# Loading the last columns of w_out first, one 8 KB row per DMA engine, in a decode step of attention and gated MLP

## The chip, the cores and the metric

The kernel runs on one core of one Trainium2 chip. The core has five engines with instruction queues of their own: TensorE (PE in the profile; its weight loads are PEld), VectorE (DVE), ScalarE (ACT), GpSimd (POOL) and SyncE (SP). Data move between the chip's memory (HBM) and the on-chip buffer by 16 DMA engines. SyncE and ScalarE issue the transfers here, each through a queue of its own; the profile calls SyncE's queue q1 and ScalarE's q10.

The metric is the device time of one execution in microseconds (us). The kernel before takes 678.6 us, the median of three runs that lie between 678.34 and 678.68.

## The reference

For eight sequences (B = 8), one new token each, with D = 512:

```
xn  = layernorm(x)
q   = xn @ wq                                   # 512 x 4096: 32 heads of 128
s   = softmax(q k^T / sqrt(128)) v  @ wo        # 8 kv heads, 4096 cached keys and values
z   = gelu(xn @ w_in)                           # 512 x 1792
z1, z2 = halves of z;  z2 = layernorm(z2) * w_sp + b_sp
g   = silu((z1 * z2) @ w_out)                   # 896 x 512
out = x + s * g
```

All of it is 32-bit floating point. The caches of keys and values are 128 MiB each, wq and wo 8 MiB each, w_in and w_out about 5.4 MB together.

## The kernel before

**Slots.** The on-chip buffer holds three slots, A, B and C, of 128 partitions x 64 KB (8 MiB each). Every large operand goes through a slot as one transfer of 128 rows of 64 KB: wq into B, then for each of the eight kv heads the first half of its keys into A, the second half into B, the first half of its values into C, the second half into B, and at the end wo into A in seven pieces (`WO_PIECES`). In the program's list the transfers of keys and values stand at lines 591 and 596, with 597 for the last quarter of the last values, and wo at 601; SyncE issues all of them in this order. A transfer into a slot is issued as soon as TensorE has made the last matmul that reads what the slot held. While SyncE waits for that, the transfers behind it in its queue wait too.

**The start.** ScalarE issues x in two halves of 8 rows (line 362) and then `w_mlp` (line 368), which holds w_in and nearly all of w_out: 128 rows of 41,984 bytes into slot C. SyncE issues wq (line 365), then `w_ext` (line 371), then the first keys (591). `w_ext` is what is missing from `w_mlp`: the last 256 columns (XN) of the last 128 rows of w_out, 128 KB. It is packed by the host: the 128 rows are cut into XC chunks of XK rows, and each partition of the transfer holds one row of every chunk side by side. Before, XK = 32 and XC = 4, so it is 32 partitions of 4 KB, seen as 8 groups (XG) of 4 rows (XR). An extra row of zeros that stands between the groups in HBM and is not loaded keeps them apart.

**The work at the start.** x is normalised (lines 419 to 427), transposed, and multiplied by wq in `project_q` (447 to 455) into the queries of all heads; this frees slot B. Then `mlp` computes the gate: w_in (469), gelu and the normalisation on VectorE and ScalarE (473 to 499), two transposes of the product (502), XC transposes of the rows that meet `w_ext` (509), the matmuls with w_out from `w_mlp` (514), and XC matmuls with `w_ext` (518). Line 518 is the last to read slot C, so the first values wait for it. Lines 520 to 531 finish the gate.

**The loop.** For each kv head: scores of the 8 sequences against both halves of the keys (550), the softmax (554 to 573), the products with the values (582 to 585), a combining matmul (588). After the eighth head wo is applied as its pieces land (609, 617), and the result is multiplied by the gate, added to x and stored (663 to 665).

**What sets the order.** Each engine executes in program order. A recorder derives the waits from which tile regions are read and written; a transfer has a semaphore that reaches 16 when all parts of it have landed.

Of the kernel before, what the change touches and what calls it, by code (L numbers as in the profile page):

```python
# [16 lines left out]
B, D = 8, 512  # L17
HKV, REP, S, DH = 8, 4, 4096, 128
NK = D // P
# [3 lines left out]
FH = 896  # L23
FQ = 256
NB = FH // P
# [11 lines left out]
E = 2  # L37
W = P // E
BANK = 512
XG, XR, XN = 8, 4, 256  # L40
XK = XG * XR
XC = P // XK
LAST = NB - 1
# [303 lines left out]
def gqa_gmlp_decode(real, x, kT, v, wq, wo, w_mlp, w_ext, out):  # L347
    nc = Recorder(real)

    def sb(name, shape, **kw):  # L350
        return real.alloc_sbuf_tensor(name, shape, F32, **kw).ap()
# [4 lines left out]
    slots = {n: sb(f"slot_{n}", [P, SLOT], align_bytes=ALIGN) for n in "ABC"}  # L356
    pbuf = sb("pbuf", [P, J * P])
    tbuf = sb("tbuf", [P, B * J * G * REP])

    xs_sb = pbuf[:B, :XW]  # L360
    for c in range(0, XW, XW // X_PARTS):
        nc.scalar.dma_start(xs_sb[:, c:c + XW // X_PARTS], x[:, c:c + XW // X_PARTS])
    x_sb = xs_sb[:, :D]

    nc.sync.dma_start(slots["B"], wq, key="B")
    wq_sb = slots["B"].rearrange("p (k n) -> p k n", k=NK)
    n_in, n_mlp = NK * 2 * FH, NK * 2 * FH + NB * D - XN
    nc.scalar.dma_start(slots["C"][:, :n_mlp], w_mlp, key="C")
    w_in_sb = slots["C"][:, :n_in].rearrange("p (k n) -> p k n", k=NK)
    ext = slots["C"][:XK, n_mlp:n_mlp + XC * XN]  # L370
    nc.sync.dma_start(ext, w_ext[:, :XR])
    w_ext_sb = ext.rearrange("p (c d) -> p c d", d=XN)

    def w_out_sb(j):
        return slots["C"][:, n_in + j * D:min(n_in + (j + 1) * D, n_mlp)]
# [163 lines left out]
    p = pbuf.rearrange("p (j s) -> p j s", j=J)  # L539
# [163 lines left out]
```

## Time and profile before

| quantity | value |
|---|---|
| median of three runs | 678.6 us (678.34 to 678.68) |
| the profiled execution | 678.58 us, of which the span from first to last instruction is 677.3 us |
| bytes read from HBM | 290.74 MB, 429 GB/s over the span |
| mean busy share of the DMA engines | 90% or more in 39 of 40 slices, 70 to 80% in the last |
| TensorE busy | 374.1 us (55%) |
| VectorE busy | 165.1 us (24%) |
| mean granted TensorE clock | 0.773 |
| packets of q1 / q10 | 6088 with 285.38 MB / 176 with 5.39 MB |

A row of a timeline has the start in us from the start of the span, the time it takes in us, engine, line, operation and tiles. SPq and ACTq are the instruction queues of SyncE and ScalarE, where issuing a transfer is an instruction of its own. The DMA view, asked for a short stretch, counts the packets that start in that stretch by queue; the percentage behind a queue is the time of those packets as a share of 16 engines over the stretch, so it passes 100% where long packets start in a short stretch. A row of a transfer is one packet; a packet of 4 bytes is the note by which one DMA engine tells the semaphore that its part is done. Such notes are the packets under 512 bytes.

### The profile page before, as it was taken

The numbers are of one execution on the slowest core, as the hardware profiler recorded it, in microseconds if no ns is written. First come the engines' busy times: TensorE is split into PE (matmuls) and PEld (weight loads), VectorE is DVE, ScalarE is ACT, GpSimd is POOL, SyncE is SP. The second block draws the span as 40 slices with busy tenths as digits, with TensorE's granted clock in tenths as the row PEclk, the third lists the DMA queues.
The fourth block names the chain that finished last, engine by engine and source line by source line (L and its number), as shares of the span: only waits on it lengthen the run. The fifth ranks groups of instructions, "written<-read, shape, count | busy, mean of one in ns | idle before, by whom it ended". The sixth has DMA issues, their size and how long they took to land. (4 is left out here: it accounts for less than half of the span.)

```text
span 677.3 us, 6190 instructions
## 1 busy us (share of the span) xinstructions
PE 374.1 (55%) x2670; PEld 120.4 (18%) x2670; DVE 165.1 (24%) x262; ACT 15.0 (2%) x35; POOL 4.4 (1%) x22
## 2 busy tenths in 40 slices
PE   0084865446665454555754464655745356655576
PEld 0031221112211121111211121111211021111222
DVE  2014133301430033401431024401422024400451
ACT  0000000000000000000000000000000000000000
POOL 1000000000000000000000000000000000000000
PEclk9996767787876667887676778877667788876688
DMA  9999999999999999999999999999999999999997
GB/s 383 435 438 434 434 434 431 434 434 437 434 434 434 434 434 434 434 434 434 434 434 434 434 434 434 434 437 434 437 441 434 434 437 434 434 437 434 427 419 310
DMA packets 6270, 290.86 MB, mean 429 GB/s; under 512 B 840, under 2 KB 856, under 8 KB 1528
## 3 DMA queue, kind: packets, MB, share of 16 engines
q1 hardware_dynamic: 6088, 285.38, 97.4%
q10 hardware_dynamic: 176, 5.39, 1.8%
q8 instruction: 5, 0.08, 0.0%
q14 instruction: 1, 0.01, 0.0%
HBM read 290.74 MB, written 0.03 MB: 429 GB/s over the span
## 5 line engine op out<-in xcount | busy, mean ns | idle before, releaser
L550 PE MATMUL sc<-slot_B,qz 128*32 128x512 f32 x512 | 72.0, 725 | 70.9 <-PEq L550 70.9
L582 PE MATMUL o_ps<-slot_B,tbuf 128*16 128x512 f32 x512 | 75.3, 715 | 62.7 <-PEq L582 62.7
L550 PE MATMUL sc<-slot_A,qz 128*32 128x512 f32 x512 | 73.8, 741 | 45.6 <-PEq L550 45.6
L582 PE MATMUL o_ps<-slot_C,tbuf 128*16 128x512 f32 x512 | 75.7, 732 | 12.6 <-PEq L582 12.6
L584 DVE TENSOR_TENSOR o_all<-o_ps,diag 128x512 f32<-128x512 f32 x64 | 44.2, 691 | 133.2 <-DVEq L584 133.2
L554 DVE TENSOR_REDUCE nm<-sc 128x1 f32<-128x1024 f32 x8 | 9.8, 1225 | 266.2 <-DVEq L554 266.2
L585 DVE TENSOR_REDUCE o_sb<-o_all 128x128 f32<-128x512 f32 x64 | 67.7, 1058 | 9.3
L550 PEld LDWEIGHTS sc<-slot_B,qz 128*32 128x32 f32 x512 | 19.9, 130 | 122.8 <-issue 122.8
L550 PEld LDWEIGHTS sc<-slot_A,qz 128*32 128x32 f32 x512 | 20.2, 133 | 92.7 <-issue 92.7
L588 PE MATMUL po<-fold,o_sb 128*128 128x4 f32 x128 | 24.2, 259 | 18.8 <-PEq L588 17.4
L588 PEld LDWEIGHTS po<-fold,o_sb 128*128 128x128 f32 x128 | 19.9, 195 | 74.3 <-issue 74.3
L582 PEld LDWEIGHTS o_ps<-slot_B,tbuf 128*16 128x16 f32 x512 | 13.4, 105 | 90.5 <-issue 90.1
L582 PEld LDWEIGHTS o_ps<-slot_C,tbuf 128*16 128x16 f32 x512 | 15.5, 112 | 53.8 <-issue 53.5
L572 PE MATMUL scr<-ident,pbuf 128*128 128x128 f32 x64 | 15.5, 424 | 13.4 <-PEq L572 13.4
L447 PE MATMUL scr<-slot_B,xnT 128*32 128x512 f32 x64 | 9.7, 761 | 19.1 <-PEq L447 19.1
L572 PEld LDWEIGHTS scr<-ident,pbuf 128*128 128x128 f32 x64 | 12.6, 224 | 13.8 <-issue 13.8
L555 ACT ACTIVATE pbuf<-sc,nm 128x1024 f32<-128x1024 f32 x8 | 8.9, 1113 | 273.5 <-DVEq L554 273.5
L573 DVE COPY tbuf<-scr 128x512 f32<-128x512 f32 x16 | 11.1, 691 | 12.4 <-DVEq L573 12.4
L558 PE MATMUL scr<-ident,nm 128*1 128x128 f32 x8 | 2.2, 269 | 13.7 <-PEq L558 13.7
L449 DVE TENSOR_SCALAR pbuf<-scr 128x512 f32<-128x512 f32 x2 | 1.4, 691 | 28.0 <-PE scr L447 28.0
L609 PE MATMUL sc<-slot_A,oT 128*8 128x512 f32 x48 | 7.8, 729 | 0.8 <-DMA slot_A<-in_wo 0.8
L565 PE MATMUL scr<-wl,same 128*128 128x1 f32 x16 | 3.6, 297 | 8.0 <-PEq L565 8.0
(105 smaller groups left out, 83.4 us busy)
## 6 DMA issues: line engine op xcount, KB each, us to landing
slot_B<-in_v SPq DMA_DIRECT2D x1, 6144.0 KB, 25.4
slot_C<-in_w_mlp ACTq DMA_DIRECT2D x1, 5248.0 KB, 35.8
slot_A<-in_wo SPq DMA_DIRECT2D x1, 3584.0 KB, 36.4
slot_B<-in_v SPq DMA_DIRECT2D x1, 2048.0 KB, 28.3
slot_A<-in_wo SPq DMA_DIRECT2D x1, 2048.0 KB, 40.8
slot_A<-in_wo SPq DMA_DIRECT2D x2, 768.0 KB, 42.9
slot_A<-in_wo SPq DMA_DIRECT2D x1, 512.0 KB, 44.3
slot_A<-in_wo SPq DMA_DIRECT2D x2, 256.0 KB, 44.6
```

Source lines behind the costliest of these rows:

```text
L447: nc.tensor.matmul(pq[R * g:R * (g + 1), :], xnT[:, k, :], wq_sb[:, k, lo:lo + REP * DH], start=(k == 0), stop=(k == NK - 1))
L550: nc.tensor.matmul(sc[R * g:R * (g + 1), c, :], qz[:, b * R:(b + 1) * R], k_sb[:, i, c, g, :], start=(b == 0), stop=(b == B - 1))
L554: nc.vector.tensor_reduce(nm, sc, op=ALU.max, axis=AX.XY, negate=True)
L555: nc.scalar.activation(p.rearrange("p j s -> p (j s)"), sc.rearrange("p c s -> p (c s)"), AF.Exp, bias=nm, accum_out=l)
L565: nc.tensor.matmul(tot, same_all, wl, start=True, stop=True)
L572: nc.tensor.transpose(t[:, j * P:(j + 1) * P], p[:, 4 * c + j, :], ident)
L573: nc.vector.tensor_copy(pT[:, :, 4 * c:4 * c + 4].rearrange("p b j (g r) -> p (j g) b r", g=G), t.rearrange("p (m b r) -> p m b r", b=B, r ...
L582: nc.tensor.matmul(of[R * c:R * c + G * REP, :], pT[:, b, j, :], v_unit[:, j], start=(j < G), stop=(j >= J - G))
L584: nc.vector.tensor_mul(o_all[b % 2], o, diag[:, :, None].to_broadcast([P, G, DH]), after=after)
L585: nc.vector.tensor_reduce(o_sb[b % 2], o_all[b % 2].rearrange("p g d -> p d g"), op=ALU.add, axis=AX.X)
L588: nc.tensor.matmul(po[:, b * REP:(b + 1) * REP], o_sb[b % 2], fold, start=True, stop=True)
L609: nc.tensor.matmul(part[R * r:R * r + B, :], oT[:, h, r, :], wo_sb[:, m, :], start=(m < REP), stop=(m >= FOLDED - REP))
```

## The change

ScalarE issues `w_ext`, and does so first of all, ahead of x and `w_mlp`. SyncE's queue has wq and behind it at once the first keys. `w_ext` is cut differently: XG, XR = 16, 1 in place of 8, 4, so that it is 16 partitions of 8 KB (XK = 16, XC = 8) with the same 128 KB. With that the loops over XC at lines 507 to 509 and 517 to 518 make 8 transposes and 8 matmuls of 16 rows in place of 4 and 4 of 32 rows.

```diff
-XG, XR, XN = 8, 4, 256
+XG, XR, XN = 16, 1, 256
 XK = XG * XR
 XC = P // XK
...
+    nc.sync.dma_start(slots["B"], wq, key="B")
+    wq_sb = slots["B"].rearrange("p (k n) -> p k n", k=NK)
+    n_in, n_mlp = NK * 2 * FH, NK * 2 * FH + NB * D - XN
+    ext = slots["C"][:XK, n_mlp:n_mlp + XC * XN]
+    nc.scalar.dma_start(ext, w_ext[:, :XR])
+    w_ext_sb = ext.rearrange("p (c d) -> p c d", d=XN)
+
     xs_sb = pbuf[:B, :XW]
     for c in range(0, XW, XW // X_PARTS):
         nc.scalar.dma_start(xs_sb[:, c:c + XW // X_PARTS], x[:, c:c + XW // X_PARTS])
     x_sb = xs_sb[:, :D]
-
-    nc.sync.dma_start(slots["B"], wq, key="B")
-    wq_sb = slots["B"].rearrange("p (k n) -> p k n", k=NK)
-    n_in, n_mlp = NK * 2 * FH, NK * 2 * FH + NB * D - XN
     nc.scalar.dma_start(slots["C"][:, :n_mlp], w_mlp, key="C")
     w_in_sb = slots["C"][:, :n_in].rearrange("p (k n) -> p k n", k=NK)
-    ext = slots["C"][:XK, n_mlp:n_mlp + XC * XN]
-    nc.sync.dma_start(ext, w_ext[:, :XR])
-    w_ext_sb = ext.rearrange("p (c d) -> p c d", d=XN)
```

The first place is the start of ScalarE's list. A row names the line, the operation, the tile written and the one read, and the partitions x elements of each.

```order
-L362 DMA pbuf<-in_x 8x288 x2
-L368 DMA slot_C<-in_w_mlp 128x10496
+L364 DMA slot_C<-in_w_ext 16x2048
+L369 DMA pbuf<-in_x 8x288 x2
+L371 DMA slot_C<-in_w_mlp 128x10496
 L477 ACT_TABLE_LOAD
 L477 ACTIVATE pbuf<-pbuf 128x512
```

`w_ext` now stands ahead of both halves of x and of `w_mlp`; line numbers moved by the edit.

The second place is TensorE's list at the end of `mlp`, from the last sum of the normalisation to the matmuls behind w_out.

```order
 L484 MATMUL scr<-var_sum,same 128x1
 L502 MATMUL scr<-ident,pbuf 128x128 x2
-L509 MATMUL scr<-ident,pbuf 32x32 x4
+L509 MATMUL scr<-ident,pbuf 16x32 x8
 L514 MATMUL sc<-slot_C,tbuf 32x512 x6
 L514 MATMUL sc<-slot_C,tbuf 32x256
-L518 MATMUL sc<-slot_C,tbuf 32x256 x4
+L518 MATMUL sc<-slot_C,tbuf 32x256 x8
 L525 MATMUL scr<-tbuf,same 32x64 x8
```

There are four transposes and four matmuls more, all ahead of the point at which slot C is free.

## The prediction

> **What bounds the kernel now.** I read the page's row of DMA shares first, then the chain that ended last, then the last stretch in small windows.
>
> ```profile
> DMA  9999999999999999999999999999999999999997
> DMA slot_A<-in_wo 7%; PE sc L550 1%; SPq L601 0%; PE sc L617 0%; SPq L597 0%; DVE res L663 0%; DVE res L664 0%; PEldq L550 0%
> ```
>
> The 16 DMA engines are busy from start to end, and the chain's largest piece is the landing of wo. No engine's arithmetic bounds the time: only the bytes, the rate, the few us before the first packet and behind the last one, and any moment in which a DMA engine has no row to fetch. The columns of the next view are stretch and length in us, busy time of PE, PEld, DVE, ACT and POOL, granted clock, DMA share and GB/s.
>
> ```profile
> 672.50:674.00 1.50, 1.25 (x88) 1.11 (x76) 0.00 (x0) 0.00 (x0) 0.00 (x0) 1.00 0.44 161
> 674.00:675.00 1.00, 0.79 (x44) 0.54 (x32) 0.00 (x0) 0.00 (x0) 0.00 (x0) 1.00 0.02 8
> 674.70 0.43 PE L617 MATMUL sc<-slot_A,oT_end 128*32 128x64 f32 x16 [0.21 <-DMA slot_A<-in_wo]
> ```
>
> The engines don't end together. After 672.5 each has on average 1.5 x 0.44 + 1.0 x 0.02 = 0.68 us of work, so a perfectly even load would end near 673.2; the last matmuls start at 674.70, when the last engine is done. Evening out the engines can therefore bring at most 1.5 us, and less if the engine that ends last is not the one relieved. Where the unevenness comes from can be counted in the landing of one transfer of keys late in the run (first 594.5 to 595.8, then 595.8 to 597.0; 40 slices each), with the instruction loads between 45 and 110 us behind it:
>
> ```profile
> DMA  0000000090990900900000990900000009000000
> DMA packets 22, 0.72 MB, mean 555 GB/s; under 512 B 11, under 2 KB 11, under 8 KB 11
> DMA  0000000000900090000900000900000900000000
> ...
> q8 instruction: 3, 0.05, 0.3%
> ```
>
> Eleven engines note their end in the first stretch (two of the nines stand for two engines each): six at 594.76 to 595.02, five at 595.22 to 595.57. Five follow at 596.10 to 596.73. An instruction load goes to one engine and delays it alone, which is my reading of the five late ones. The gap between the six and the five is what an uneven small transfer leaves.
>
> **The change part by part.**
>
> *The bytes of w_ext per engine.* These are DMA views of 31.0 to 31.8 us, and of 34.4 to 35.4 us:
>
> ```profile
> q1 hardware_dynamic: 8, 0.03, 9.9%
> ...
> DMA packets 47, 1.05 MB, mean 1049 GB/s; under 512 B 16, under 2 KB 16, under 8 KB 32
> q1 hardware_dynamic: 39, 1.05, 243.0%
> q10 hardware_dynamic: 8, 0.00, 0.5%
> ```
>
> Eight rows of 4 KB take 9.9% of 16 x 0.8 us, which is 0.158 us each. In the second view 16 notes end: 8 are q10's, the others q1's notes for w_ext. So eight engines carry it, four rows each: 0.63 us more than the other eight. They also carry x's 16 rows (below). The change gives every engine two times 4 KB, 0.32 us: these eight end 0.32 us earlier, the others 0.32 us later, the mean stays. In the landing above, six plus two of the late five would be the engines without w_ext, five plus three those with it, the last among them. Then the last goes from 596.73 to 596.41, while the later of the other two late ones, near 596.22, comes to 596.54. **The end moves by 596.54 - 596.73 = -0.2 us**; the bounds are -0.32 us (all late ones relieved) and +0.32 us (the last is one without w_ext).
>
> [...]
>
> *The turns at the start.* The stretches are 7.2 to 7.9 and 9.6 to 10.4 us, and then comes the use of x:
>
> ```profile
> DMA packets 24, 0.87 MB, mean 1242 GB/s; under 512 B 0, under 2 KB 8, under 8 KB 8
> q10 hardware_dynamic: 16, 0.35, 114.5%
> ...
> DMA packets 16, 0.52 MB, mean 655 GB/s; under 512 B 8, under 2 KB 8, under 8 KB 8
> q1 hardware_dynamic: 8, 0.52, 151.1%
> ...
> 10.64 0.68 DVE L419 BATCH_NORM_STATS2 st<-pbuf 8x6 f32<-8x512 f32 x1 [6.98 <-DMA pbuf<-in_x]
> ```
>
> A row of wq takes 151.1% of 16 x 0.8 us by eight, 2.42 us. At 7.2 us eight engines make x's second rows, while the other eight already make w_mlp's first; at 9.6, one row of wq later, x's eight notes. So each engine alternates between the two queues row by row, and a note costs a turn of 2.42 us like a row. With w_ext ahead, x's first half comes a place later, so on x's engines two more turns (its row and its note) stand before w_mlp: about 4.8 us. x is in use at 15.5 in place of 10.6 us. That is covered by wq, which TensorE can't have before 33.69 (next fence). Of the eight rows that w_mlp has on each of these engines, the first four now go beside wq's fifth to eighth and the rest beside the 4 KB rows of w_ext. After the change the first two go beside wq's seventh and eighth, two follow there, and five rows of the first keys come between the rest and its note: + 5 x 2.42 - 3 x 0.16 + 0.32 = 11.9 us.
>
> ```profile
> 33.69 6.07 PE L447 MATMUL scr<-slot_B,xnT 128*32 128x512 f32 x32 [19.05 <-PEq L447]
> 47.43 3.65 PE L469 MATMUL scr<-slot_C,xnT 128*32 128x256 f32 x64 [1.16 <-DVE scr L463]
> ...
> 62.10 0.39 PE L509 MATMUL scr<-ident,pbuf 32*32 32x32 f32 x4
> 66.13 1.91 PE L518 MATMUL sc<-slot_C,tbuf 32*32 32x256 f32 x8
> 71.29 9.48 PE L550 MATMUL sc<-slot_A,qz 128*32 128x512 f32 x64 [2.04 <-PEq L550]
> 80.58 7.05 PE L550 MATMUL sc<-slot_B,qz 128*32 128x512 f32 x64
> ```
>
> The eight engines in question end their part of w_mlp between 34.4 and 35.4 now: that view has their notes. These would come at 46.3 to 47.3. TensorE can begin line 469 at 47.43 + 0.32 (wq lands later by w_ext's share) = 47.75. It fits, by 0.4 us at the worst: the cover is project_q, and one turn more costs 2.42 us less that 0.4.
>
> *The matmuls.* Line 518 doubles: 8 records, 1.91 us, so +1.91 (up to +3.8 should the clock be half there). Line 509 gets four more transposes, about +0.2. The copy at line 510 stays beside line 514's matmuls. With wq's 0.32 the release of slot C and the scores behind it come 2.4 us later. What waits for that is SyncE (ahead of its issues a DMA view of 1.6 to 1.744 us, where q10 is alone, one of 1.6 to 2.3, and one of 53.4 to 55.3, where the first keys land):
>
> ```profile
> q10 hardware_dynamic: 7, 0.01, 11.8%
> ...
> q1 hardware_dynamic: 15, 0.98, 423.1%
> ...
> DMA packets 30, 0.98 MB, mean 517 GB/s; under 512 B 15, under 2 KB 15, under 8 KB 15
> ...
> 0.74 0.39 SPq L365 DMA_DIRECT2D slot_B<-in_wq  x1
> ...
> 44.86 0.33 SPq L591 DMA_DIRECT2D slot_B<-in_kT  x1
> 68.07 0.33 SPq L596 DMA_DIRECT2D slot_C<-in_v  x1
> 87.94 0.33 SPq L596 DMA_DIRECT2D slot_B<-in_v  x1
> ```
>
> The first keys end from 53.5 us on, the second half 8 x 2.42 = 19.3 later, at 72.8, and the first values at 92.1. From an issue to its packets 1.0 to 1.6 us pass (wq: issue at 0.74, packets at 1.74 to 2.3). So the issue at 68.07 has 72.8 - 1.0 - 68.1 = 3.7 us of slack and the one at 87.94 has 3.2, or 0.6 less on the engines served last. With 2.4 us used, 1.3 and 0.8 are left: cost nothing, and 1.1 at the upper bound of 4.3. That SyncE no longer issues w_ext frees nothing: the keys issued behind it wait for wq's rows anyway.
>
> *Sum:* 678.58 (profiled, the median is 678.6) - 0.2 + 0 + 0 = **678.4 us**.
>
> [...]
>
> **The rivals.** *Nothing to gain:* the engine that ends last carries no w_ext, or a load of instructions falls elsewhere; 678.6 to 678.9. For it: which engines the five late ones are I inferred from groups alone. Against: the two groups of six and five, which only w_ext and x can have parted.
>
> [...]
>
> *It isn't split as meant:* w_ext stays on eight engines; 678.6.
> *w_mlp comes too late:* if on one engine wq's row is taken before w_ext's, a turn is lost, 2.4 us. Line 469 starts at 49.7, so 2.4 + 2.0 = 4.4 us of slack are used: 0.7 too many at the first issue, 1.2 in all at the second, 679.1 to 679.6. With two turns lost it is 2.4 more, some 681.8. It decides from a landing after 47.75 + 0.8. For it: the fit is close. Against: x's first rows, issued where w_ext's are now, came before wq's on most of the eight engines (q10 alone until 1.744), and none of the eight shows a lost turn at 7.2.
> *Evener than I think:* all the unevenness goes, 677.1 to 677.6. Against: five engines are late by loads that no edit here moves.
>
> **How the numbers follow.** Forecast 0.66 (own range 678.1 to 678.7), nothing to gain 0.10, not split 0.04, one turn lost 0.09, two or more 0.05, evener 0.06. A measurement tells about 0.2%, 1.36 us, from no change. Faster than 677.2: part of the last, 0.04. Slower than 680.0: two turns and the worst of one, 0.07. Same: 0.89. The range, 677.8 to 679.7, leaves out the evener case and two turns lost.
>
> **What would show it.** Sixteen packets of 8 KB in the first half microsecond of q10, all ahead of wq's; x in use near 15.5; line 469 near 47.7 with no wait for slot C; line 518 with 16 records in 3.8 us; issues to slots C and B near 70.5 and 90; DMA shares of 1.0 from 72 to 94 us; the notes of later keys in two groups closer together. I am wrong if line 469 waits for DMA, if shares dip near 73 or 92 us, or if the last wo piece lands later than 674.7.

## The result, and the profile after

The changed kernel takes **686.8 us** (median of six runs, 682.4 to 688.1), the kernel before beside it on the same chip 678.6 us. The medians differ by 8.2 us, where 678.4 us was forecast and 677.8 to 679.7 was the range. The ratio over all executions is 1.0106, with a 95% interval of 1.0086 to 1.0125, which is 5.8 to 8.5 us: two of the six executions took 682.4 and 683.4. The profiled execution took 686.85 us with a span of 685.5, against 678.58 and 677.3: 8.3 and 8.2 us, so the trace has the loss in it. Of all the executions below one, of 776.7 us (the old order with two rows an engine), was in a slower state of the chip and is left out of the ratios.

The page of the kernel after shows where. The rows are the granted TensorE clock, the DMA share and the rate in 40 slices, each 17.1 us long, and a transfer's size with the time from its issue to its landing:

```profile
PEclk9995598887687767777787767777778777777789
DMA  9999699999999999999999999999999999999997
GB/s 381 436 424 429 245 429 430 428 440 451 444 428 429 428 432 436 428 428 428 432 455 444 428 432 428 436 432 428 428 428 451 451 428 432 428 436 432 413 441 312
slot_C<-in_w_mlp ACTq DMA_DIRECT2D x1, 5248.0 KB, 48.7
```

The same rate row of the kernel before:

```profile
GB/s 383 435 438 434 434 434 431 434 434 437 434 434 434 434 434 434 434 434 434 434 434 434 434 434 434 434 437 434 437 441 434 434 437 434 434 437 434 427 419 310
```

The fifth slice (68.5 to 85.7 us) moved 245 in place of 434 GB/s: 0.44 of 17.1 us, 7.5 us. The third and fourth add 0.5 and 0.2 us. These slices hold about all of the 8.2 us; the rest of the run is nearly as fast as before.

What the DMA engines did there stands in the windows of the kernel after (stretch and length, busy time of PE, PEld, DVE, ACT, POOL, granted clock, DMA share, GB/s):

```profile
68.00:72.00 4.00, 4.00 (x24) 1.01 (x23) 0.84 (x2) 0.00 (x0) 0.00 (x0) 0.50 1.13 492
72.00:76.00 4.00, 4.00 (x11) 1.48 (x10) 0.00 (x0) 0.00 (x0) 0.00 (x0) 0.50 0.12 49
76.00:80.00 4.00, 3.52 (x9) 1.11 (x7) 0.44 (x1) 0.00 (x0) 0.00 (x0) 0.50 0.00 0
80.00:84.00 4.00, 1.65 (x24) 0.82 (x28) 1.44 (x5) 0.26 (x1) 0.00 (x0) 0.50 1.31 492
```

A packet counts in the window in which it starts. Only three rows start from 72 to 76 us, the last at 73.3, and none from there to 80.5. Most engines began their last row of the keys near 71.6 and ended it 2.42 us later, near 74; their next row starts near 80.6, so they have nothing to fetch for about 6.6 us. TensorE is busy nearly all that time, at half clock. The timeline of the kernel after shows with what (start, duration, engine, line, operation and tiles, idle time ahead of it and what ended that):

```profile
19.21 0.68 DVE L419 BATCH_NORM_STATS2 st<-pbuf 8x6 f32<-8x512 f32 x1 [15.55 <-DMA pbuf<-in_x]
50.91 6.43 PE L469 MATMUL scr<-slot_C,xnT 128*32 128x256 f32 x64 [4.17 <-PEq L469]
68.93 3.63 PE L514 MATMUL sc<-slot_C,tbuf 128*32 128x512 f32 x14
72.49 7.03 PE L518 MATMUL sc<-slot_C,tbuf 16*32 16x256 f32 x16
79.55 0.33 SPq L596 DMA_DIRECT2D slot_C<-in_v  x1
99.35 0.33 SPq L596 DMA_DIRECT2D slot_B<-in_v  x1
682.88 0.43 PE L617 MATMUL sc<-slot_A,oT_end 128*32 128x64 f32 x16 [0.21 <-DMA slot_A<-in_wo]
```

The first values are issued at 79.55 in place of 68.07, 11.48 us late. Three pieces make that up: line 469 starts 50.91 - 47.43 = 3.48 us late; it takes 6.43 in place of 3.65, 2.78 more; line 518 takes 7.03 in place of 1.91, 5.12 more. (The last 0.1 us is spread between them.) The slack at that issue was 3.7 us by the prediction's count, 0.6 less on the engines served last, so that 7.8 to 8.4 us come out at the end. The longer rows of w_ext's neighbours, below, add nothing to that here: they make the keys late, and the dry moment is shorter by as much (the keys' last rows end near 74.0 in place of 72.8, and 6.6 + 1.2 = 7.8).

Line 469 waits for w_mlp, which lands 48.7 us after its issue at 2.09, at 50.8. How it came to be that late is in the order of the first rows: DMA views of the kernel after for 1.6 to 4.7, 4.7 to 5.9 and 6.5 to 9.0 us (packets, MB, their time as a share of 16 engines):

```profile
q1 hardware_dynamic: 16, 1.05, 100.9%
...
q1 hardware_dynamic: 15, 0.98, 248.0%
q10 hardware_dynamic: 15, 0.12, 28.6%
...
q1 hardware_dynamic: 16, 1.05, 97.3%
q10 hardware_dynamic: 15, 0.00, 0.3%
```

Until 4.7 us there are only wq's sixteen first rows. The 8 KB rows of w_ext start behind them, on all engines, and their notes another row later. The prediction had w_ext ahead of wq, as x's first rows had been on most engines. That the order at the start isn't settled could be seen in the kernel before: x's second half, issued together with the first, came only at 7.2 us, behind two rows of wq. The second view shows a second thing that was not foreseen: wq's second rows take 248.0% x 19.2 us / 15 = 3.17 us each, where they took 2.42 before; the third rows are back at 97.3% x 40 / 16 = 2.43. (wq's very first rows take 3.1 us or more in both kernels.) So the rows that run beside w_ext lose 0.75 us. That it goes with w_ext and not with the hour is borne out by the kernel in which w_ext stands between x's halves and starts behind two rows of wq: there wq's second rows take 2.43 us and its third, beside w_ext, 229.9% x 20.8 / 15 = 3.19 (7.0 to 8.3 us):

```profile
q1 hardware_dynamic: 15, 0.98, 229.9%
q10 hardware_dynamic: 16, 0.13, 29.9%
```

### The profile page after: what moved, and what is told of

Same layout as the page of the kernel before. It is cut to its first block, busy times and chain, and to the rows that moved or that the text cites. A ratio compares the mean times of both kernels' runs of the same rounds, so it can differ in the third digit from the quotient of the medians.

```text
span 685.5 us, 6214 instructions
## 1 busy us (share of the span) xinstructions
PE 383.5 (56%) x2682; PEld 133.5 (19%) x2682; DVE 165.4 (24%) x262; ACT 15.0 (2%) x35; POOL 4.4 (1%) x22
## 5 line engine op out<-in xcount | busy, mean ns | idle before, releaser
L550 PEld LDWEIGHTS sc<-slot_A,qz 128*32 128x32 f32 x512 | 29.9, 132 | 83.4 <-issue 82.2
L582 PEld LDWEIGHTS o_ps<-slot_C,tbuf 128*16 128x16 f32 x512 | 15.5, 112 | 53.6 <-issue 53.3
L572 PE MATMUL scr<-ident,pbuf 128*128 128x128 f32 x64 | 15.5, 423 | 13.4 <-PEq L572 13.4
L469 PE MATMUL scr<-slot_C,xnT 128*32 128x256 f32 (+1 forms) x64 | 6.4, 548 | 4.2 <-PEq L469 4.2
## 6 DMA issues: line engine op xcount, KB each, us to landing
slot_C<-in_w_mlp ACTq DMA_DIRECT2D x1, 5248.0 KB, 48.7
```

Of the source, the lines that this page charges most:

```text
L469: nc.tensor.matmul(pz[R * g:R * (g + 1), part * FQ:part * FQ + n], xnT[:, k, :], w_in_sb[:, k, part * FH + lo:part * FH + lo + n], start=( ...
L550: nc.tensor.matmul(sc[R * g:R * (g + 1), c, :], qz[:, b * R:(b + 1) * R], k_sb[:, i, c, g, :], start=(b == 0), stop=(b == B - 1))
L572: nc.tensor.transpose(t[:, j * P:(j + 1) * P], p[:, 4 * c + j, :], ident)
L582: nc.tensor.matmul(of[R * c:R * c + G * REP, :], pT[:, b, j, :], v_unit[:, j], start=(j < G), stop=(j >= J - G))
```

## The experiments

Four questions: what the lost turns cost, what the doubled matmuls and the clock cost, what the new cut of w_ext costs alone, and whether even engines are worth anything. The edits of code are against the kernel before or after, as stated. Every ratio is to runs of the kernel before on the same chip; its medians there lay between 678.2 and 678.7 us. The last three columns are of the one execution that was profiled. For w_ext between x's halves (684.8 us) and for the idle time filled (685.7 us) that was the slowest one, 2.4 and 1.8 us above the median.

| kernel | median us | ratio, 95% interval | line 469 starts, takes | line 518 takes | first values issued |
|---|---|---|---|---|---|
| before | 678.6 | 1 | 47.43, 3.65 | 1.91 | 68.07 |
| after | 686.8 | 1.0106 (1.0086 to 1.0125) | 50.91, 6.43 | 7.03 | 79.55 |
| after, x in one piece | 679.5 | 1.0015 (1.0005 to 1.0025) | 47.33, 3.65 | 3.86 | 69.97 |
| before, x in one piece | 678.6 | 1.0000 (0.9991 to 1.0010) | 47.31, 3.65 | 1.91 | 67.92 |
| move alone, old cut | 688.0 | 1.0144 (1.0129 to 1.0158) | 57.50, 5.24 | 1.91 | 79.82 |
| move, two rows an engine | 687.2 | 1.0133 (1.0118 to 1.0147) | 55.45, 6.09 | 2.29 | 79.02 |
| after, w_ext between x's halves | 682.4 | 1.0056 (1.0039 to 1.0072) | 48.57, 6.49 | 7.03 | 77.26 |
| after, w_ext last | 680.1 | 1.0027 (1.0017 to 1.0036) | 47.52, 3.65 | 3.88 | 70.14 |
| after, half the matmuls | 682.7 | 1.0056 (1.0041 to 1.0072) | 51.09, 5.48 | 1.99 | 73.71 |
| after, wait filled | 683.1 | 1.0063 (1.0040 to 1.0086) | 52.78, 3.65 | 3.94 | 75.35 |
| x in one piece, idle time added | 683.4 | 1.0070 (1.0047 to 1.0092) | 50.29, 5.96 | 3.94 | 75.40 |
| the same, idle time filled | 683.9 | 1.0068 (1.0048 to 1.0088) | 50.04, 3.65 | 7.03 | 75.92 |
| new cut alone | 680.3 | 1.0026 (1.0016 to 1.0035) | 48.25, 3.65 | 3.84 | 70.88 |
| old order, two rows an engine | 679.4 | 1.0013 (1.0004 to 1.0022) | 47.35, 3.65 | 1.91 | 67.76 |
| new cut alone, spread out | 679.0 | 1.0008 (0.9999 to 1.0018) | 48.01, 3.65 | 3.70 | 70.61 |
| 8 KB rows on eight engines | 679.5 | 1.0036 (1.0011 to 1.0061) | 48.05, 3.65 | 3.80 | 70.68 |
| w_out whole, no w_ext | 678.5 | 1.0000 (0.9991 to 1.0009) | 47.65, 3.65 | none | 66.53 |

### The turns

Two edits take turns away from the queue ahead of w_mlp, one from the kernel after, one from the kernel before as a control:

```diff
-X_PARTS = 2
+X_PARTS = 1
```

> The changed kernel with x issued in one piece in place of two (8 rows of 2304 bytes): two turns less ahead of w_mlp on eight engines. Turn theory: x is in use near 14.4 us instead of 19.2, w_mlp lands 4.8 us earlier, near 46, so line 469 starts near 48 with project_q as what ends its wait; slot C is issued at 71.5 to 75.5 depending on the granted clock, and the time is 679.4 to 682 us. If the wait of line 469 is not set by turns, w_mlp lands near 50.8 as in the changed kernel and the time stays near 686.

> The kernel before with x in one piece: two turns less ahead of w_mlp on eight engines, where nothing waits for them. Turn theory: w_mlp's rows start 4.8 us earlier there, line 469 still starts near 47.4 because project_q ends its wait, and the time does not move: 678.4 to 678.8 us. It tells whether the gain of one piece in the changed kernel comes from the turns alone.

x in one piece needs one row and one note less on each of its eight engines. In the kernel after, w_mlp then lands at 1.78 + 44.3 = 46.1 us and 7.3 of the 8.2 us come back; in the kernel before, where w_mlp lands at 1.66 + 35.8 = 37.5 and has 10 us to spare, nothing changes. The timeline of the kernel after with x in one piece shows the whole chain in time:

```profile
47.33 3.65 PE L469 MATMUL scr<-slot_C,xnT 128*32 128x256 f32 x64 [1.16 <-DVE scr L463]
66.08 3.86 PE L518 MATMUL sc<-slot_C,tbuf 16*32 16x256 f32 x16
69.97 0.33 SPq L596 DMA_DIRECT2D slot_C<-in_v  x1
```

So the mechanism was one of turns and of their cover, and not of bytes.

Next, the move alone, with w_ext cut as before, and the move with another cut (16, 2):

```diff
-XG, XR, XN = 16, 1, 256
+XG, XR, XN = 8, 4, 256
```

```diff
-XG, XR, XN = 16, 1, 256
+XG, XR, XN = 16, 2, 256
```

> The move alone: ScalarE issues w_ext first, but still cut as 8 groups of 4 rows of 4 KB, so line 518 has 8 records again. Turn theory: on eight engines four rows and a note of w_ext take five turns where the changed kernel has two, w_mlp's last row falls behind four or more further rows of keys, w_mlp lands at 58 to 62 us instead of 50.8, line 469 starts there, slot C is issued near 79 to 82, and the time is 685 to 689 us. Matmul theory: line 518 takes 1.9 to 3.5 us, slot C is issued at 68 to 70, 678.4 to 679 us.

> The move with the even cut that keeps 4 matmuls: 16 groups of 2 rows of 4 KB, issued by ScalarE first of all. Turn theory: three turns for w_ext on each engine instead of two, so w_mlp lands 2.4 us later than in the changed kernel, near 53.2, line 469 starts there, line 518 takes 1.9 to 3.5 us, slot C is issued at 74 to 78.5 and the time is 680.5 to 685 us. Matmul theory: 678.3 us, since line 518 is as before.

The move alone loses the most: four rows and a note on the x engines are five turns, and w_mlp lands at 57.3, a little ahead of what was expected. Two rows an engine were expected to lose less than they did. There w_ext's rows came only behind wq's *second* rows, one more turn; line 469 started at 55.45 and took 6.09 us (granted clock 0.50 from 48 to 56 us, 0.67 from 56 to 66). How many rows of wq pass first went with the length of ScalarE's issue instruction: 0.41 us for one row an engine (behind the first), 0.69 and 1.27 us for two and four (behind the second). That x's eight short rows had passed ahead of wq with a start at the same moment was not explained by any run.

Two orders on ScalarE's queue keep the new cut. In one, w_ext stands between x's halves, in the other behind w_mlp:

```diff
-    nc.scalar.dma_start(ext, w_ext[:, :XR])
...
         nc.scalar.dma_start(xs_sb[:, c:c + XW // X_PARTS], x[:, c:c + XW // X_PARTS])
+        if c == 0:
+            nc.scalar.dma_start(ext, w_ext[:, :XR])
```

```diff
-    nc.scalar.dma_start(ext, w_ext[:, :XR])
...
     nc.scalar.dma_start(slots["C"][:, :n_mlp], w_mlp, key="C")
     w_in_sb = slots["C"][:, :n_in].rearrange("p (k n) -> p k n", k=NK)
+    nc.scalar.dma_start(ext, w_ext[:, :XR])
```

> The changed kernel, but ScalarE issues w_ext between the two halves of x instead of ahead of both; everything else as in the change. Turn theory: on x's eight engines the first half of x and its note pass ahead of wq as in the kernel before, so one pair of turns less stands ahead of w_mlp than in the changed kernel. That is the row order the prediction assumed: w_mlp lands at 46 to 48.5 us in place of 50.8, line 469 starts at 47.4 to 48.6, slot C is issued at 70 to 72, and only the slowing of long rows beside w_ext is left: 679.2 to 680.3 us. If place in the queue is not what counts (some other part of the change delays w_mlp), w_mlp lands near 50.8 and the time is 682 to 688 us.

> The changed kernel with w_ext issued last by ScalarE, behind x and w_mlp; the cut of 16 rows of 8 KB and the 8 matmuls stay. Turn theory: x and w_mlp have their turns of before, w_mlp lands near 37.5 us and line 469 starts near 47.5; the doubled line 518 (3.8 us at full clock) lets slot C be issued at 70 to 71, within its slack, so no moment without DMA near 73 us. What remains is the slowing of long rows beside w_ext (0.8 us per engine in the changed kernel, 1.7 in the recut alone): 679.3 to 680.4 us. If the doubled matmuls are what costs: slot C at 73 or later and 682 or more.

With w_ext last nothing is late, as expected, and 1.6 us are lost all the same (more on that below). With w_ext between the halves, x's first half passes ahead of wq and w_mlp lands at 48.5, one turn ahead of the kernel after. That is about the order on which the prediction's own number rested, and still w_mlp is 1.2 us or more later than the 46.3 to 47.3 of the prediction; the row beside w_ext accounts for 0.75 of it. It was expected to cost 0.6 to 1.7 us and cost 3.8 (four executions, 681.4 to 684.8), by the lower clock on lines 469 and 518 (granted 0.50 from 48 to 52 us, 0.70 from 52 to 56, 0.50 from 68 to 76; timeline of the slowest, line numbers one higher than in the kernel after):

```profile
48.57 6.49 PE L470 MATMUL scr<-slot_C,xnT 128*32 128x256 f32 x64 [3.80 <-PEq L470]
70.20 7.03 PE L519 MATMUL sc<-slot_C,tbuf 16*32 16x256 f32 x16
77.26 0.33 SPq L597 DMA_DIRECT2D slot_C<-in_v  x1
```

So even the forecast's own order of rows would have lost about 4 us.

### The matmuls and the clock

Four of the eight chunks of w_ext are left out of lines 509 and 518 of the kernel after:

```diff
-        for c in range(XC):
+        for c in range(XC // 2):
...
-                             start=False, stop=(c == XC - 1))
+                             start=False, stop=(c == XC // 2 - 1))
```

> The changed kernel, but only the first four of the eight chunks are transposed and multiplied (lines 509 and 518 have 8 records again; half of the last columns' contribution is left out). The turns at the start are those of the changed kernel. Turn theory with the matmuls as an addition: line 469 still starts near 50.9 and, where the clock is half, takes 6.4 us; line 518 takes 1.9 to 3.5 in place of 7.0, slot C is issued near 75 to 76 and the time is 3 to 4 us less, 682.5 to 684 us, still 4 us or more above before. If the doubled matmuls were the cause by themselves: 679.4 us.

As expected, 4.1 of the 8.2 us come back. They aren't the price of four matmuls alone: line 518 took 0.25 us a record here, against 0.44 in the kernel after and 0.24 in the kernel before, and line 469 in 5.48 us in place of 6.43, so that the first values were issued earlier (73.71) than the 75 to 76 expected. Of the kernels in the table with eight matmuls of w_ext (16 records in line 518), three had them at 0.44 us a record, the kernel after among them, and the others at 0.23 to 0.25. The windows of before and after show the difference (48 to 56 and 66 to 70 us, before 56 to 66 as well; the granted clock is the third number from the end). Before:

```profile
48.00:56.00 8.00, 3.09 (x58) 1.68 (x51) 3.97 (x7) 0.63 (x1) 0.00 (x0) 0.98 0.94 403
56.00:66.00 10.00, 5.50 (x24) 2.10 (x24) 3.70 (x13) 0.00 (x0) 0.73 (x2) 0.50 1.00 433
66.00:70.00 4.00, 2.47 (x26) 1.03 (x24) 1.05 (x3) 0.26 (x1) 0.00 (x0) 0.92 1.10 475
```

After:

```profile
48.00:56.00 8.00, 5.09 (x51) 2.82 (x53) 0.00 (x0) 0.00 (x0) 0.00 (x0) 0.61 0.94 403
66.00:70.00 4.00, 2.28 (x18) 1.10 (x21) 2.03 (x5) 0.00 (x0) 0.53 (x2) 0.50 1.17 508
```

(The row for 66 to 70 us of the kernel after ends line 509 and begins 514; line 518 follows at 0.50 as well, in the windows above.) The clock is at half from line 484 on in the kernel before too (0.50 from 56.12 to 62.69 us), and line 514 runs at 0.53 there. What differs is that it is full again (1.00) when line 518 starts.

Whether the wait itself takes the clock away, or only the later hour, was tried with three kernels. The first fills the wait of the kernel after with 24 matmuls on data that are there; the second adds idle time to the kernel with x in one piece, in which no transfer is late; the third fills that idle time.

```diff
         nc.vector.memset(pz, 0.0)
+        for _ in range(24):
+            nc.tensor.matmul(sc[:, 1, :P], ident, ident, start=True, stop=True)
         for part in range(2):
```

```diff
-        nc.vector.memset(pz, 0.0)
+        for _ in range(6):
+            nc.vector.memset(pz, 0.0)
```

```diff
         for _ in range(6):
             nc.vector.memset(pz, 0.0)
+        for _ in range(22):
+            nc.tensor.matmul(sc[:, 1, :P], ident, ident, start=True, stop=True)
```

> The changed kernel, with 24 matmuls of 128x128 (identity by identity, into an unused bank) put ahead of line 469, so that TensorE works for some 4 us while it waits for w_mlp. The result is unchanged. Theory that TensorE's idle time brings the half clock: line 469 (now line 471) starts near 51 as in the changed kernel (50.91) but runs in 3.7 to 4.5 us instead of 6.43; what follows comes at least 2 us earlier, the first values are issued by 77.5, and the profiled run takes 684.5 or less, less still if line 518 also meets the full clock. Rival, that the clock falls by its own schedule or by the mere time: line 469 takes 6.4 us again, the issue stays at 79.5, the time at 686 to 687.

> The changed kernel with x in one piece, in which w_mlp comes in time, and in which VectorE clears the result bank of line 469 six times in place of once, so that TensorE idles 2.5 us longer ahead of it with every DMA in time. The result is unchanged. Theory that TensorE's idle time brings the half clock: line 469 starts near 49.9 and takes some 6.4 us instead of 3.65, line 518 some 7 instead of 3.86; the first values are issued near 69.97 + 2.5 + 2.8 = 75.3 or, with line 518 slow as well, 78.4; 682 to 685.5 us. Rival, that only a late DMA goes with it, or that the clock follows another schedule: 3.65 and 3.86 us, issue near 72.5, 679.5 to 680.2 us.

> As the kernel with the bank cleared six times, and in the added idle time 22 matmuls of 128x128 on data that are already there. The result is unchanged. Theory that idle time and not the late start brings the half clock: line 469 starts near 49.9 and takes 3.65 to 4.2 us; the first values are issued near 72.5 to 73.5; 679.5 to 681 us. Rival, that the later start alone does it: 6.4 us as without the filling.

Timeline of the kernel with the wait filled (line numbers two higher than in the kernel after; the trace counts two records for a filling matmul):

```profile
45.71 5.52 PE L465 MATMUL sc<-ident 128*128 128x128 f32 x48
52.78 3.65 PE L471 MATMUL scr<-slot_C,xnT 128*32 128x256 f32 x64 [1.54 <-PEq L471]
71.38 3.94 PE L520 MATMUL sc<-slot_C,tbuf 16*32 16x256 f32 x16
```

Of the kernel with idle time added (one higher):

```profile
50.29 5.96 PE L470 MATMUL scr<-slot_C,xnT 128*32 128x256 f32 x64 [4.50 <-DVE scr L464]
71.42 3.94 PE L519 MATMUL sc<-slot_C,tbuf 16*32 16x256 f32 x16
```

Of the kernel with that idle time filled (three higher):

```profile
50.04 3.65 PE L472 MATMUL scr<-slot_C,xnT 128*32 128x256 f32 x64
68.86 7.03 PE L521 MATMUL sc<-slot_C,tbuf 16*32 16x256 f32 x16
```

For line 469 the theory of the idle time holds in all three. Filled, it runs in 3.65 us although it starts at 52.78, later than in the kernel after (w_mlp came 1.8 us later in that run); the first values are issued 4.2 us earlier and the median falls by 3.7 us, as expected (the three executions lie between 682.7 and 683.4, where two of the six of the kernel after lie too, so that the rows show it better than the times). With idle time added, where VectorE's clearing and no transfer ends the wait, it slows to 5.96. The kernel takes 3.9 us more than the one with x in one piece; the first values are issued 5.43 us later there, 2.96 by the added idle time itself and 2.31 by the slower line 469. Over all kernels in the table: idle for 0 to 1.54 us ahead of it, 3.65 us; idle for 3.80 us or more, 5.24 to 6.49 us.

For line 518 the theory was not enough. The expectation had 7 us with idle time added and 3.9 with it filled; it came out the other way round, and the third kernel's 683.9 us missed its 679.5 to 681. Its eight executions fall into two groups, three of 681.3 to 681.6 and five of 683.5 to 685.7 us, and the rows above are of the slowest; whether line 518 was fast in the first group no trace shows. What decides whether the clock is full by the time of line 518 stays open. In the windows of the kernel after TensorE is busy for 4.00 of 4.00 us from 68 to 72 and again to 76, and the clock stays at 0.50.

### The new cut alone

The kernel before, with w_ext cut into 16 rows of 8 KB (the new cut), and into two rows for each of 16 engines, both issued by SyncE where it stood:

```diff
-XG, XR, XN = 8, 4, 256
+XG, XR, XN = 16, 1, 256
```

```diff
-XG, XR, XN = 8, 4, 256
+XG, XR, XN = 16, 2, 256
```

> The recut alone: 16 rows of 8 KB, but issued by SyncE behind wq as before, so ScalarE's queue is as before. Turn theory (the loss comes from w_mlp landing late, because w_ext and x take turns ahead of it): w_mlp lands near 37.5 us, line 469 starts at 47.4 to 47.8, slot C is issued at 70 to 73 (68.07 plus 1.9 to 5.1 for the doubled line 518), within its slack of 3.7, so 678.2 to 679.5 us. Matmul theory (the doubled line 518 alone outruns the slack, 7.03 us against 1.91): issue at 73.2 or later, DMA idle near 73 and 92 us, 680 to 683 us.

> Evening out alone: w_ext as 16 groups of 2 rows of 4 KB (32 partitions, 4 matmuls as before), issued by SyncE behind wq as before. If the balance of the engines is worth what the prediction said: all 16 engines carry two rows, line 518 keeps 8 records and 1.9 us, slot C is issued near 68 us, the last engine ends 0.2 us earlier, 678.3 us (678.0 to 678.6). If w_ext on all engines costs something of its own (the first 20 us show rows of 3.2 us in place of 2.42 beside it): up to 0.8 us slower, 679.4.

The cut alone costs 1.6 us, though the first values were issued in time (70.88) and no share dipped near 73 us: the theory of the matmuls falls here. The first keys are late instead: 15 of their 16 notes come at 55.4 to 56.0 us, where 14 came at 53.4 to 54.4 before. The DMA views show the rows that became longer. New cut alone, 31 to 32 us (w_mlp's rows are q10's, w_ext's q1's):

```profile
q10 hardware_dynamic: 16, 0.67, 220.9%
q1 hardware_dynamic: 8, 0.07, 17.7%
```

The kernel before, 30.8 to 31.8 us:

```profile
q10 hardware_dynamic: 16, 0.67, 155.2%
q1 hardware_dynamic: 8, 0.03, 8.0%
```

Sixteen rows of w_mlp beside w_ext take 220.9% x 16 / 16 = 2.21 us each instead of 1.55. Two rows for each engine lost 0.7 us in the same way, with smaller pieces (a row of w_mlp took 1.78 us at 32.6 to 33.6 us).

Is it the number of engines, or where the rows are written? The next kernel writes the 16 rows to every eighth partition instead of the first sixteen. (Its matmuls read other columns, so that part of the result is left out.) The one after it gives 8 engines two rows of 8 KB each, to the first 16 partitions.

```diff
-XG, XR, XN = 8, 4, 256
+XG, XR, XN = 16, 1, 256
...
-    ext = slots["C"][:XK, n_mlp:n_mlp + XC * XN]
-    nc.sync.dma_start(ext, w_ext[:, :XR])
-    w_ext_sb = ext.rearrange("p (c d) -> p c d", d=XN)
+    nc.sync.dma_start(slots["C"][::P // XK, n_mlp:n_mlp + XC * XN], w_ext[:, :XR])
+    w_ext_sb = slots["C"][:XK, :XC * XN].rearrange("p (c d) -> p c d", d=XN)
```

```diff
-XG, XR, XN = 8, 4, 256
+XG, XR, XN = 8, 2, 256
```

> The recut alone (16 rows of 8 KB, issued by SyncE behind wq), but the 16 rows are written to every 8th partition, 0, 8, ... 120, instead of partitions 0 to 15. The matmuls of line 518 then read columns of w_in in place of the last columns of w_out, so that part of the result is left out; their number and size stay. Destination theory (long rows slow down because 16 engines write into few partitions that other rows are also bound for): the excess of long rows over 2.42 and 1.55 us near 31 to 36 us, 1.7 us per engine in the recut alone, falls to half or less, and the time goes from 680.3 to 679.3 or less. Size theory (small rows on all 16 engines at once slow the next rows wherever they go): excess and time as in the recut alone, 680.3.

> The recut to 16 partitions of 8 KB, but as 8 groups of 2 rows, so that 8 engines carry it as before the change, issued by SyncE behind wq. Destination theory: engine e writes partitions 2e and 2e+1 in place of 4e to 4e+3, all within the first 16, so long rows slow down although only 8 engines carry w_ext: an excess of 0.8 to 1.7 us per engine and 679.3 to 680.5 us. Size theory or a theory that 16 engines have to take part: no excess, 678.6 us as before (line 518 doubles, but within its slack).

Spread out, 31.0 to 32.4 us:

```profile
q10 hardware_dynamic: 16, 0.67, 124.0%
q1 hardware_dynamic: 8, 0.07, 11.1%
```

124.0% x 22.4 / 16 = 1.74 us a row, and 1.2 of the 1.6 us come back, with the same bytes from the same place and the same number of rows. With eight engines and the first 16 partitions a row of w_mlp is 131.6% x 22.4 / 16 = 1.84 us, and 0.9 us stay lost, though some runs of that kernel scattered up to 685.7. So the destination is a cause, but not the only one: into the same 16 partitions, rows from eight engines cost less than rows from sixteen (1.84 against 2.21 us). Why the destination counts no run shows, nor which engine writes which partition. Against 2.42 and 1.55 us, a long row beside w_ext was 0.75 us longer in the kernel after, 0.66 with the new cut alone, 0.29 with eight engines and 0.19 with the rows spread out. With the old cut, 32 rows of 4 KB from eight engines to 32 partitions, the rows beside it grew neither in the kernel before (1.55 us) nor with the move alone (2.42 us for a row of wq beside w_ext).

### Even engines

w_out is loaded whole with w_mlp, 128 rows of 43,008 bytes; w_ext and its matmuls are gone (the edit is shortened here):

```diff
-    n_in, n_mlp = NK * 2 * FH, NK * 2 * FH + NB * D - XN
+    n_in, n_mlp = NK * 2 * FH, NK * 2 * FH + NB * D
...
-        for c in range(XC):
-            nc.tensor.matmul(sc[R * g:R * (g + 1), 0, D - XN:], hX[:, c, :], w_ext_sb[:, c, :],
-                             start=False, stop=(c == XC - 1))
```

> No w_ext at all: w_mlp is loaded whole, 128 rows of 43,008 bytes, so the same 128 KB go to all 16 engines and each engine writes the partitions that it writes in every 128-row transfer. Lines 509, 510 and 518 are gone, line 514 has a full last matmul. Destination theory: no long row slows down (excess near 0 apart from the first rows), the keys' notes lie in one group apart from the late ones, and what is left is what the balance was forecast to bring: 0.2 to 0.4 us, 678.2 to 678.4 us. If even shares on 16 engines slow the long rows for another reason than the destination: 679 us or more.

With w_out in the 128 even rows of w_mlp, and rows of 64 KB at 2.42 us (96.7% x 40 / 16, 34.5 to 37 us), the time is that of the kernel before within 0.1%; the 0.2 to 0.4 us expected didn't show. The last matmuls start at 674.66, before at 674.70:

```profile
674.66 0.43 PE L603 MATMUL sc<-slot_A,oT_end 128*32 128x64 f32 x16 [0.20 <-DMA slot_A<-in_wo]
```

In that execution the end was as late without w_ext's uneven rows as with them, so they weren't what set it. The times alone can't exclude a gain of 0.2 us: their interval is 0.6 us to either side. None of the kernels was faster than the kernel before beyond that.

## Why the prediction was wrong

**What bounds the kernel: right.** The time goes by the bytes and by the moments in which the engines have no row. The one such moment came where it was placed, at the first issue to slot C, with the slack that was counted there.

**The bytes per engine: the split right, the worth wrong.** That 16 rows would go to 16 engines no row of the kernel before had shown; in the kernel after 16 rows of w_ext, 0.13 MB, start from 4.7 to 6.5 us, and 16 notes follow from 8.2 to 9.5. No run shows the term of -0.2 us: it came out at about 0 with w_out whole (the last matmuls 0.04 us earlier, the median 0.1 us lower, within 0.6 us of noise). Which engines end last had been inferred from two groups of notes; that instruction loads make five of them late was the author's reading, which no run tried.

**The turns at the start: the failing step.** "Each engine alternates between the two queues row by row, and a note costs a turn" held once both queues were running (in the kernel after w_ext's rows from 4.7 us on, its notes from 8.2, one row of wq later). That w_ext would pass ahead of wq, as x's first rows did, didn't: wq's rows came first on all engines, so that one more turn stood before w_mlp, and the row beside w_ext was 0.75 us longer. x was in use at 19.21 in place of 15.5, w_mlp's last notes came at 50.8 in place of 46.3 to 47.3. "It fits, by 0.4 us" was the step on which all hung; a margin of a sixth of a turn on an order that one row of the profile supported. The order was not all of it: with about the forecast's order restored w_mlp landed at 48.5, still past the 47.75 at which line 469 could have begun. The lost turn is the rival "w_mlp comes too late", with a chance of 0.09.

**The price of being late: mis-sized, in the rival too.** The rival gave 679.1 to 679.6 us, by a lateness of 2.4 and line 518's +2.0. Measured were 3.48 for the start, +2.78 for line 469, which was counted at nothing, and +5.12 for line 518, for which +1.91 was taken and +3.8 was the bound. The prediction held the clock of the kernel before as fixed. Line 469's part is shown to come from the wait: a wait at one place made the work behind it 1.4 to 1.8 times as long (5.24 to 6.49 in place of 3.65 us). Why line 518 lost the clock stays open. 5.12 exceeds even the bound, which had doubled only the added 1.91: at half clock (0.50) all 16 records slow down, 0.44 us each in place of 0.24, not only the eight that were added.

**Matmuls without lateness: right.** Where w_mlp is in time, the issue comes at 70 to 71 us as forecast (70.5) and no row is missed.

**The cost of the cut: left out.** No term had the longer rows beside w_ext: 0.7 to 1.6 us by the kernels that change the cut alone. With w_mlp in time the change would still have ended near 679.5, where x in one piece ends.

**The tests it named** gave the answer: line 469 waited, the shares dipped near 73 us, and the last piece of wo landed later than 674.7.

## What to carry to other kernels

With two queues at work here, a transfer of a few KB cost turns, not bytes: one row and one note per engine, each as long as the row that the other queue had there (2.42 us; with x in one piece, two turns less, w_mlp landed 4.7 us earlier). Count such turns against the cover of what stands behind, and want at least one whole turn of margin where the order of the first rows is inferred. Price a possible lateness with the clock that TensorE has after a wait: here a wait of 4 us made the 32 matmuls behind it (64 records) take 1.8 times as long.

Before splitting a small load over more engines, ask what it does to the long rows beside it, and whether evenness was what set the end: here it cost 0.7 to 1.6 us and brought nothing that could be measured.

## What the runs showed of the hardware that was not expected

- Long rows were slower beside w_ext's 8 KB rows to the first 16 partitions: 3.17 in place of 2.42 us for 64 KB, 2.21 in place of 1.55 for 41,984 bytes; 1.84 with 8 KB rows from eight engines, 1.74 where the 8 KB rows were spread over the partitions.
- The granted clock at line 469 went with TensorE's idle time ahead of it: up to 1.54 us of it the line took 3.65 us (1.00 in the kernel before), from 3.80 us on 5.24 to 6.49 (0.50 at its start and 0.56 over the whole line in the kernel after). At line 518 of the kernel after it was 0.50 although TensorE had been busy for more than 4 us; why is open. That may be why the late kernels scatter (682.4 to 688.1 for the kernel after), while most of those in time stay within 0.3%; but 8 KB rows on eight engines scattered too (679.0 to 685.7), and no trace shows why.
- Which of two queues with a first transfer at the same moment is served first changed with the transfer: eight rows of x ahead of wq (most by 1.74 us), 16 rows of 8 KB behind its first rows (from 4.7 us), two or four rows an engine behind its second (from 7.2 us). This order was seen, not explained.
